# Two-layer squared-ReLU kernel: column-tiled warm-up, natural weight group only in block 0, no loads on the GpSimd queue

## The chip, the cores and the metric

The kernel runs on one core of one Trainium2 chip. The metric is the device time in microseconds (us), lower is better. Most executions of a kernel agree within 0.3%, so a change of a few tenths of a microsecond in 291 is read from repeated runs and, above all, from the trace, where single instructions have start times. All runs quoted here are with a granted TensorE clock of 0.999 to 1.0 in the mean.

Names: PE is TensorE, PEld its weight loads (LDWEIGHTS), ACT is ScalarE, DVE is VectorE, POOL is GpSimd, SP is SyncE. A name with a q at the end is that engine's sequencer, which issues DMAs. A *slot* is the time from the start of one 512-column matmul to the start of the next; w1n is the natural group's weight tile, loaded in slices of the contraction rows (four of 128 and a short one of 64, in two halves), w_h and w_x in the views are the row-pair weights `w1_h` and `w1_x`.

## The reference

```python
B, S, D, F = 1, 2048, 576, 4608          # all bf16
h = einsum("bsd,df->bsf", x, w1) + b1    # (2048, 4608)
h = relu(h) ** 2
out = einsum("bsf,fd->bsd", h, w2) + b2  # (2048, 576)
```

## The kernel before

The 2048 rows are cut into 4 blocks of 512. For each block, the first layer makes 36 tiles of 128 hidden features ("phase A"); for two blocks at a time the second layer follows. D is 576 = 9 x 64, so a tile needs 4.5 passes of 128 contraction rows. The kernel avoids the half-empty pass in two ways:

- 32 of the 36 tiles are made in *row pairs*: one tile in array rows 0 to 63 and another in rows 64 to 127, nine 64-row matmuls each, running side by side. A pair takes 9 slots. Its two weight halves come as two loads, "lower" and "upper".
- the other 4 tiles, the *natural group*, use 4 full 128-row passes each plus one 64-row pass shared by two: 16 + 2 = 18 slots for four tiles, as many as two row pairs.

```python
WARM = [512] * 6 + [128]
for i, n in enumerate(WARM):                      # keeps PE busy until x lands
    matmul(wps[:, 0:n], lhsT=ones[:, 0:P], rhs=ones[:, 0:n], start=True, stop=True)
# loads: x tiles 0, 3 and w1n slices 0..3 on SyncE, x tiles 1, 2 on ScalarE
...
nc.gpsimd.dma_start(out=b1_rows[0:NFT, :], in_=b1...)          # b1
for h in range(2):
    nc.gpsimd.dma_start(out=b2_col[h*DT:(h+1)*DT, :], in_=b2...)  # b2, twice 64 x 2 B
...
def a_rows(sb, ...):                              # row pairs j = 0..15
    for j in range(NJ):
        bx, by = psum(), psum()
        for i in range(NC):                       # 9 slots, two matmuls side by side
            matmul(bx, lhsT=w1_h[0:H, LO_C[i], jc], rhs=xT[0:H, LO_W[i], :])
            matmul(by, lhsT=w1_h[H:P, UP_C[i], jc], rhs=xT[H:P, UP_W[i], :])
        evac_h(sb, bx, G + j); evac_h(sb, by, G + NJ + j)   # ACT relu+b1, DVE square
# row weights, on SyncE, one lower and one upper load for each range of pairs:
# (0,1) w1n rest (1,2) (2,4) (4,6) (6,8) (8,10) (10,12) x block 1 (12,14) (14,16)
...
a_full(0, "k_outer"); a_rows(0, 12, 1)            # block 0: natural group first
a_rows(1); a_full(1, "rows_first")                # block 1: natural group last
phase_t(0)                                        # last 64 output columns, transposed
phase_b(0, ...); phase_b(1, ...)                  # the other 512 output columns
a_full(2, "g_outer"); a_rows(2)                   # block 2: natural group first
a_rows(3); a_full(3, "rows_first")                # block 3: natural group last
phase_t(2); phase_b(2, ...); phase_b(3, ...)
```

## Time and profile before

| | before |
|---|---|
| time, median of 3 runs | 291.73 us (291.54 to 291.87) |
| span of the profiled run | 289.8 us |
| PE busy | 285.1 us, 98% |
| one 512-column slot, start to start | 0.2157 us |

The page of the kernel before: the head, PE's busy time, and the chain that ended last by engine.

```profile
span 289.8 us, 4679 instructions
...
PE 285.1 (98%) x2017; PEld 133.7 (46%) x2032; DVE 79.5 (27%) x176; ACT 95.2 (33%) x152; POOL 2.8 (1%) x11
...
q0 software_dynamic: 96, 0.01, 0.0%
...
PE 98%; issue 0%; DVE 0%
```

The chain is PE from end to end: whatever is to be gained must be taken from PE's own sequence. The q0 line is the GpSimd queue with the three small loads (96 packets).

The timeline of the kernel before, PE only (start, duration, engine, line, operation, names, shapes), at the end of phase A of block 1: row pairs, natural group, transposed output.

```profile
72.16 0.38 PE L191 MATMUL ph<-xTw,w_h 64*128 64x512 bf16 x1
72.38 0.38 PE L204 MATMUL pn<-xTw,w1n 64*128 64x512 bf16 x1
72.38 0.38 PE L206 MATMUL pn<-xTw,w1n 64*128 64x512 bf16 x1
72.59 0.38 PE L204 MATMUL pn<-xTw,w1n 64*128 64x512 bf16 x1
72.59 0.38 PE L206 MATMUL pn<-xTw,w1n 64*128 64x512 bf16 x1
73.13 3.40 PE L210 MATMUL pn<-xTw,w1n 128*128 128x512 bf16 x15 [0.16 <-issue]
76.46 0.84 PE L272 MATMUL pt<-hT,w_sb 128*64 128x512 bf16 x6
```

From 72.38 to 76.46 are 4.08 us for 18 slots of 0.2157 us (3.88 us). The 0.20 us over are two changes of tile shape: 64-row tiles to the full array, and the full array to 64-column tiles. (The group shows 15 of 16 matmuls: the record of one beside such a change is missing.)

The start of the kernel before in PE's timeline: warm-up, transposes of x, first matmuls.

```profile
0.77 2.83 PE L63 MATMUL wps<-const-bfloat16-1.0 128*128 128x512 bf16 x7 [0.77 <-PEq L346]
3.49 1.25 PE L150 MATMUL tb<-ident,x_sb 128*128 128x128 bf16 x10
4.59 1.01 PE L228 MATMUL pn<-xTw,w1n 128*128 128x256 bf16 x4
```

Ten 128-column transposes from 3.49 to 4.59 are 0.11 us each; after 6.65 us the spacing in the trace is 0.056 us. PE works at half speed up to there. Below, this step from half to full speed is called the opening of the clock gate.

### The profile page before, as it was taken

To read this page: it belongs to the slowest core of one execution; us is meant where nothing else is said; L and a number is where in the kernel's file an instruction comes from. 1 tells how busy PE (TensorE), PEld (TensorE's weight loads), DVE (VectorE), ACT (ScalarE), POOL (GpSimd) and SP (SyncE) were. 2 spreads that over 40 slices of the span, in tenths; PEclk is the share of its full clock that TensorE was granted. 3 is DMA by queue.
4 is the path that set the end of the run, shared out by engine and by line. 5 is a ranking of instruction groups with operands and counts; after the bars stand their busy time and mean duration, and the time that the engine had idled before them with its cause. 6 is when DMAs were issued, how large, how long until landed. Compare 5 with 4: busy or idle time off the path is not lost.

```text
span 289.8 us, 4679 instructions
## 1 busy us (share of the span) xinstructions
PE 285.1 (98%) x2017; PEld 133.7 (46%) x2032; DVE 79.5 (27%) x176; ACT 95.2 (33%) x152; POOL 2.8 (1%) x11
## 2 busy tenths in 40 slices
PE   8999999999999999999999999999999999999996
PEld 5544444444444444444444444444445444444454
DVE  1644554444502100000025444444440000000001
ACT  2666666666500000000027666666670000000000
POOL 3000000000000000000000000000000000000000
PEclk9999999999999999999999999999999999999999
DMA  7999999400001000000000000000000200000000
GB/s 198 213 235 185 315 388 234 83 0 2 0 19 33 5 20 18 18 18 20 18 18 2 1 2 0 2 0 2 0 2 0 38 18 18 18 20 18 20 18 20
DMA packets 30581, 16.26 MB, mean 56 GB/s; under 512 B 14676, under 2 KB 30560, under 8 KB 30560
## 3 DMA queue, kind: packets, MB, share of 16 engines
q1 hardware_dynamic: 30176, 15.65, 21.7%
q8 instruction: 16, 0.26, 0.4%
q10 hardware_dynamic: 288, 0.30, 0.4%
q14 instruction: 5, 0.04, 0.0%
q0 software_dynamic: 96, 0.01, 0.0%
HBM read 11.36 MB, written 2.36 MB: 47 GB/s over the span
## 4 chain that ended last, share of the span: by engine, by line
PE 98%; issue 0%; DVE 0%
PE po L293 43%; PE ph L189 42%; PE pt L272 5%; PE pn L210 4%; PE pn L228 1%; PE wps L63 1%; PE tb L150 1%; PE ph L191 1%; PE pn L204 1%; DVE o_sb L295 0%; PE b1T_ps L167 0%; PE pn L206 0%
## 5 line engine op out<-in xcount | busy, mean ns | idle before, releaser
L191 PE MATMUL ph<-xTw,w_h 64*128 64x512 bf16 x576 | 124.6, 376 | 0.0
L189 PE MATMUL ph<-xTw,w_h 64*128 64x512 bf16 x576 | 124.6, 376 | 0.0
L293 PE MATMUL po<-w_sb,hT 128*128 128x512 bf16 (+2 forms) x600 | 123.8, 366 | 0.8 <-issue 0.3
L177 ACT ACTIVATE r<-ph,b1T 128x512 bf16<-128x512 f32 x128 | 81.0, 684 | 41.7 <-PE ph L191 41.7
L293 PEld LDWEIGHTS <-hT 128*128 128x128 bf16 x612 | 58.3, 98 | 66.7 <-issue 0.8
L189 PEld LDWEIGHTS <-w_h 64*128 64x128 bf16 x576 | 54.1, 94 | 68.3
L178 DVE TENSOR_TENSOR hT<-r 128x512 bf16<-128x512 bf16 x144 | 61.1, 425 | 75.9 <-ACT r L177 75.4
L191 PEld LDWEIGHTS <-w_h 64*128 64x128 bf16 x576 | 54.1, 94 | 0.0
L295 DVE TENSOR_TENSOR o_sb<-po,b_bc 128x512 bf16<-128x512 f32 (+2 forms) x17 | 11.2, 660 | 125.0 <-PE po L293 125.0
L177 ACT ACTIVATE r<-pn,b1T 128x512 bf16<-128x512 f32 x16 | 10.3, 687 | 68.7 <-PE pn L206 67.4
L272 PE MATMUL pt<-hT,w_sb 128*64 128x512 bf16 x144 | 15.9, 380 | 0.0
L272 PEld LDWEIGHTS <-w_sb 128*64 128x64 bf16 x144 | 8.0, 110 | 7.8 <-issue 0.8
L210 PE MATMUL pn<-xTw,w1n 128*128 128x512 bf16 x45 | 10.4, 379 | 0.4 <-issue 0.3
L210 PEld LDWEIGHTS <-w1n 128*128 128x128 bf16 x48 | 4.5, 98 | 6.0 <-issue 0.8
L275 ACT ACTIVATE oT<-pt,b2T 128x512 bf16<-128x512 f32 x2 | 1.4, 687 | 14.5 <-PE pt L272 14.5
L228 PE MATMUL pn<-xTw,w1n 128*128 128x256 bf16 x32 | 4.8, 304 | 0.0
L228 PEld LDWEIGHTS <-w1n 128*128 128x128 bf16 x32 | 3.4, 110 | 0.6
L63 PE MATMUL wps<-const-bfloat16-1.0 128*128 128x512 bf16 (+1 forms) x7 | 2.8, 581 | 0.8 <-PEq L346 0.8
L157 DVE COPY xTw<-tb 128x256 bf16<-128x256 bf16 x4 | 1.1, 292 | 6.6 <-PE tb L150 6.6
L120 DVE COPY xTw<-xTw 64x2048 bf16<-64x2048 bf16 x4 | 2.8, 690 | 0.2
L121 DVE COPY xTw<-xTw 64x2048 bf16<-64x2048 bf16 x4 | 2.7, 687 | 0.1
L159 ACT COPY xTw<-tb 128x256 bf16<-128x256 bf16 x4 | 1.3, 375 | 3.7 <-PE tb L150 3.7
(23 smaller groups left out, 16.9 us busy)
## 6 DMA issues: line engine op xcount, KB each, us to landing
w_sb<-in_w_dram SPq DMA_DIRECT2D x6, 864.0 KB, 9.6
w_h<-in_w_dram SPq DMA_DIRECT2D x14, 288.0 KB, 6.8
out_dram<-o_sb SPq DMA_DIRECT2D x15, 128.0 KB, 1.7
w_h<-in_w_dram SPq DMA_DIRECT2D x4, 144.0 KB, 3.6
w1n<-in_w_dram SPq DMA_DIRECT2D x4, 128.0 KB, 3.7
x_sb<-in_x_dram ACTq DMA_DIRECT2D x2, 144.0 KB, 2.8
x_sb<-in_x_dram SPq DMA_DIRECT2D x2, 144.0 KB, 3.3
out_dram<-ot SPq DMA_DIRECT2D x4, 64.0 KB, 1.8
```

The lines of the kernel that those rows point to most:

```text
L63: keep(nc.tensor.matmul(wps[:, 0:n], lhsT=ones[:, 0:P], rhs=ones[:, 0:n], start=True, stop=True))
L150: keep(nc.tensor.transpose(bank[:, slot, qc], xs[:, j, c0:c0 + P], ident[:]))
L177: keep(nc.scalar.activation(out=r[:], in_=bank[:], func=ACT.Relu, bias=b1T[:, ft:ft + 1], scale=1.0))
L178: keep(nc.vector.tensor_tensor(out=hTs[sb][:, ft, :], in0=r[:], in1=r[:], op=ALU.mult))
L189: keep(nc.tensor.matmul(bx[:], lhsT=w1_h[0:H, LO_C[i], jc], rhs=xT[0:H, LO_W[i], :], start=(i == 0), stop=(i == NC - 1)))
L191: keep(nc.tensor.matmul(by[:], lhsT=w1_h[H:P, UP_C[i], jc], rhs=xT[H:P, UP_W[i], :], start=(i == 0), stop=(i == NC - 1)))
L204: keep(nc.tensor.matmul(banks[2 * i][:], lhsT=w1n8[0:H, i, :], rhs=xT[0:H, SPC, :], start=start, stop=stop, skip_group_check=order == "k_o ...
L210: keep(nc.tensor.matmul(banks[g][:], lhsT=w1n[:, k, g * P:(g + 1) * P], rhs=xT[:, O + k, :], start=start, stop=stop))
L228: keep(nc.tensor.matmul(banks[g][:, hc], lhsT=w1n[:, k, g * P:(g + 1) * P], rhs=xT[:, O + k, hc], start=(h == 0 and k == 0), stop=False, s ...
L272: keep(nc.tensor.matmul(pt[h * DT:(h + 1) * DT, :], lhsT=w2_sb[:, ft, DM:D], rhs=hTs[sb + h][:, ft, :], start=(i == 0), stop=(i == NFT - 1)))
L293: keep(nc.tensor.matmul(po[:, 0:d1 - d0], lhsT=hT[:, ft, jj * P:(jj + 1) * P], rhs=w2_sb[:, ft, d0:d1], start=(i == 0), stop=(i == NFT - 1)))
L295: keep(nc.vector.tensor_tensor(out=o_sb[:, d0:d1], in0=po[:, 0:d1 - d0], in1=b2_bc[:, d0:d1], op=ALU.add))
```

## The change

The intent, as the diff shows it: the same array work with fewer changes of shape (the natural group stays in block 0 alone; in blocks 1 to 3 its four tiles become two more row pairs with their own weight tile `w1_x`), a warm-up in four 32-column tiles, and no load on the GpSimd queue. w2 comes in 9 chunks in place of 6. Cut to its core:

```diff
-    WARM = [512] * 6 + [128]
-    for i, n in enumerate(WARM):
-        keep(nc.tensor.matmul(wps[:, 0:n], lhsT=ones[:, 0:P], rhs=ones[:, 0:n], start=True, stop=True))
+    WARM = [512] * 6 + [64]
+    for n in WARM:
+        for c in range(0, P, 32):
+            keep(nc.tensor.matmul(wps[c:c + 32, 0:n], lhsT=ones[:, 0:32], rhs=ones[:, 0:n], start=True, stop=True))
...
-    nc.gpsimd.dma_start(out=b1_rows[0:NFT, :], in_=b1.rearrange("(ft p) -> ft p", p=P))
-    b2_col = ...; for h in range(2): nc.gpsimd.dma_start(out=b2_col[...], in_=b2[...])
+    nc.scalar.dma_start(out=b1_rows[0:NFT, :], in_=b1.rearrange("(ft p) -> ft p", p=P))
...
-    W2CH = 6
+    W2CH = 4
...
-        for j in range(NJ):
+        pairs = [] if sb == 0 else [(w1_x, j, j, G // 2 + j) for j in range(G // 2)]
+        pairs += [(w1_h, j, G + j, G + NJ + j) for j in range(NJ)]
+        for n, (w, j, fa, fb) in enumerate(pairs):
...                                             # a_full becomes a_first, block 0 only
+    for h in range(2):
+        load_w1x(nc.sync, h)                    # after the last row weights
+    for h in range(2):
+        keep(nc.sync.dma_start(out=b2_col[...], in_=b2[...]))
...
     a_rows(1)
-    a_full(1, "rows_first")
     phase_t(0)
...
-    a_full(2, "g_outer")
     a_rows(2)
...
     a_rows(3)
-    a_full(3, "rows_first")
```

More of the change, by code (lines that the diff above doesn't have):

```diff
@@ L68 @@
     w1_h = wpool.tile([P, NC, FH], BF16, name="w1_h")
+    w1_x = wpool.tile([P, NC, GW // 2], BF16, name="w1_x")
     w1_v = w1.rearrange("(c p) f -> p c f", p=H)
@@ L83, in load_w1, with load_w1x @@
                       in_=w1_v[:, :, GW + h * FH + j0 * P:GW + h * FH + j1 * P]))
+    def load_w1x(eng, h):
+        keep(eng.dma_start(out=w1_x[h * H:(h + 1) * H, :, :], in_=w1_v[:, :, h * GW // 2:(h + 1) * GW // 2]))
     load_x(nc.sync, 0)
@@ L97 @@
     nc.gpsimd.memset(b1_rows[:], 0.0)
-    nc.gpsimd.dma_start(out=b1_rows[0:NFT, :], in_=b1.rearrange("(ft p) -> ft p", p=P))
-    b2_col = const.tile([P, 1], BF16, name="b2_col")
-    for h in range(2):
-        nc.gpsimd.dma_start(out=b2_col[h * DT:(h + 1) * DT, :], in_=b2[DM:D].rearrange("(d o) -> d o", o=1))
-    b2T = const.tile([P, 1], FP32, name="b2T")
-    nc.gpsimd.tensor_copy(out=b2T[:], in_=b2_col[:])
+    nc.scalar.dma_start(out=b1_rows[0:NFT, :], in_=b1.rearrange("(ft p) -> ft p", p=P))
     warm = const.tile([P, 1], FP32, name="warm")
@@ L181, in a_rows @@
         xT = xT_blk[sb]
-        for j in range(NJ):
-            if j == dup_at:
+        pairs = [] if sb == 0 else [(w1_x, j, j, G // 2 + j) for j in range(G // 2)]
+        pairs += [(w1_h, j, G + j, G + NJ + j) for j in range(NJ)]
+        for n, (w, j, fa, fb) in enumerate(pairs):
+            if n == dup_at:
                 dup_windows(dup_sb)
@@ L188, in a_rows @@
             for i in range(NC):
-                keep(nc.tensor.matmul(bx[:], lhsT=w1_h[0:H, LO_C[i], jc], rhs=xT[0:H, LO_W[i], :],
+                keep(nc.tensor.matmul(bx[:], lhsT=w[0:H, LO_C[i], jc], rhs=xT[0:H, LO_W[i], :],
                                  start=(i == 0), stop=(i == NC - 1)))
-                keep(nc.tensor.matmul(by[:], lhsT=w1_h[H:P, UP_C[i], jc], rhs=xT[H:P, UP_W[i], :],
+                keep(nc.tensor.matmul(by[:], lhsT=w[H:P, UP_C[i], jc], rhs=xT[H:P, UP_W[i], :],
                                  start=(i == 0), stop=(i == NC - 1)))
-            evac_h(sb, bx, G + j)
@@ L194, in a_rows, with a_first, part @@
-            evac_h(sb, by, G + NJ + j)
-    def a_full(sb, order):
-        xT = xT_blk[sb]
-        banks = []
-        for g in range(G):
-            pool, tag = (ps_o, "po") if g < 2 else (ps_h, "ph")
-            banks.append(pool.tile([P, SB], FP32, name="pn", tag=tag))
-        def pair(i, start, stop):
+            evac_h(sb, bx, fa)
+            evac_h(sb, by, fb)
+    def a_first():
+        xT = xT_blk[0]
+        banks = [ps_o.tile([P, SB], FP32, name="pn", tag="po") for _ in range(2)]
+        banks += [ps_h.tile([P, SB], FP32, name="pn", tag="ph") for _ in range(2)]
+        tb_new = [ps_h.tile([P, 2, HS], BF16, name="tb", tag="ph") for _ in range(2)]
+        half_banks[1] = tb_new + tb_po
+        def part(h, k):
+            hc = slice(h * HS, (h + 1) * HS)
+            for g in range(G):
+                keep(nc.tensor.matmul(banks[g][:, hc], lhsT=w1n[:, k, g * P:(g + 1) * P], rhs=xT[:, O + k, hc],
+                                      start=(h == 0 and k == 0), stop=False, skip_group_check=True))
+        for j in range(2):
+            for k in range(NK):
+                x_transpose(j, k)
+        for j in range(2):
+            x_transpose(j, NK)
+        x_copies(0)
+        part(0, 0)
+        for k in range(NK + 1):
+            x_transpose(2, k)
+        part(0, 1)
+        part(0, 2)
+        for k in range(NK + 1):
+            x_transpose(3, k)
+        x_copies(1)
+        dup_windows(0)
+        part(0, 3)
+        part(1, 0)
+        make_b1T()
+        for k in range(1, NK):
+            part(1, k)
+        for i in (1, 0):
@@ L204, in pair @@
             keep(nc.tensor.matmul(banks[2 * i][:], lhsT=w1n8[0:H, i, :], rhs=xT[0:H, SPC, :],
-                             start=start, stop=stop, skip_group_check=order == "k_outer"))
+                                  start=False, stop=True, skip_group_check=True))
             keep(nc.tensor.matmul(banks[2 * i + 1][:], lhsT=w1n8[H:P, i, :], rhs=xT[H:P, E3, :],
-                             start=start, stop=stop, skip_group_check=order == "k_outer"))
-        def full(g, k, start, stop):
-            keep(nc.tensor.matmul(banks[g][:], lhsT=w1n[:, k, g * P:(g + 1) * P], rhs=xT[:, O + k, :],
-                             start=start, stop=stop))
@@ L213, in a_full @@
-        if order == "rows_first":
-            for i in (1, 0):
-                pair(i, True, False)
-            for g in (2, 3, 0, 1):
-                for k in range(NK):
-                    full(g, k, False, k == NK - 1)
-                evac_h(sb, banks[g], g)
-        else:
-            if order == "k_outer":
-                tb_new = [ps_h.tile([P, 2, HS], BF16, name="tb", tag="ph") for _ in range(2)]
-                half_banks[1] = tb_new + tb_po
-                def part(h, k):
-                    hc = slice(h * HS, (h + 1) * HS)
-                    for g in range(G):
-                        keep(nc.tensor.matmul(banks[g][:, hc], lhsT=w1n[:, k, g * P:(g + 1) * P],
-                                              rhs=xT[:, O + k, hc], start=(h == 0 and k == 0), stop=False,
-                                              skip_group_check=True))
-                for j in range(2):
-                    for k in range(NK):
-                        x_transpose(j, k)
-                for j in range(2):
-                    x_transpose(j, NK)
-                x_copies(0)
-                part(0, 0)
-                for k in range(NK + 1):
-                    x_transpose(2, k)
-                part(0, 1)
-                part(0, 2)
-                for k in range(NK + 1):
-                    x_transpose(3, k)
-                x_copies(1)
-                dup_windows(0)
-                part(0, 3)
-                part(1, 0)
-                make_b1T()
-                for k in range(1, NK):
-                    part(1, k)
-            else:
-                for g in (2, 3, 0, 1):
-                    for k in range(NK):
-                        full(g, k, k == 0, False)
-            for i in (1, 0):
-                pair(i, False, True)
-                evac_h(sb, banks[2 * i], 2 * i)
-                evac_h(sb, banks[2 * i + 1], 2 * i + 1)
@@ L261 @@
+                                  start=False, stop=True, skip_group_check=True))
+            evac_h(0, banks[2 * i], 2 * i)
+            evac_h(0, banks[2 * i + 1], 2 * i + 1)
     ft_order = list(range(G))
@@ L263 @@
         ft_order += [G + j, G + NJ + j]
-    t_order = ft_order[G:] + ft_order[:G]
     EDGES = [0, 384, 512]
@@ L269, in phase_t @@
         pt = ps_o.tile([P, SB], FP32, name="pt", tag="po")
-        for i, ft in enumerate(t_order):
+        for i, ft in enumerate(ft_order):
             for h in range(2):
@@ L307 @@
         load_w1(nc.sync, 1, j0, j1)
+    for h in range(2):
+        load_w1x(nc.sync, h)
+    b2_col = const.tile([P, 1], BF16, name="b2_col")
+    for h in range(2):
+        keep(nc.sync.dma_start(out=b2_col[h * DT:(h + 1) * DT, :], in_=b2[DM:D].rearrange("(d o) -> d o", o=1)))
+    b2T = const.tile([P, 1], FP32, name="b2T")
+    nc.gpsimd.tensor_copy(out=b2T[:], in_=b2_col[:])
     keep(nc.sync.dma_start(out=b2_bc[:], in_=b2.partition_broadcast(P)))
-    for c in (0, 3, 1, 4, 2, 5):
+    for c in (0, 1, 5, 2, 6, 3, 7, 4, 8):
         load_w2(c)
@@ L313 @@
     alloc_hT(0)
-    a_full(0, "k_outer")
+    a_first()
     a_rows(0, 12, 1)
```

## The prediction

> **What bounds the kernel now.** TensorE. The page has PE busy 98% of 289.8 us at a granted clock of 1.0; the chain of waits is 98% PE. In the timeline every 512-column slot starts 0.2157 us after the one before, whether it is one 128x128 matmul or two 64-row ones side by side.
>
> **What moves without changing the sum.** The natural group is 16 full and 2 paired slots: 18 slots, 3.88 us. In blocks 1 to 3 it becomes two row pairs, 2 x 9 = 18 slots. The extra LDWEIGHTS are hidden (0.09 us inside a slot).
>
> **What is removed.** Switches of tile shape. The Trainium skill, "TensorEngine Tiling (Array Packing)", "Key Properties", says a change of mode drains the engine; the trace agrees and gives the price. From the first natural pair of block 1 (72.38) to the first matmul of the transposed output (76.46) is 4.08 us against 3.88 for 18 slots: two switches, 0.10 us each. In block 2 the one switch back costs 0.105 us (146.52 to 150.51, 18 slots). Blocks 1 and 3 lose one switch each; block 2 only moves it. Gain: 0.2 us, all on the chain.
>
> **Start.** Warm-up runs from 0.77; six matmuls 0.427 us apart and a short one end as x tile 0 lands (3.45); transposes start at 3.49. Four 32-column tiles should run side by side, as the two 64-column tiles do in the transposed output (72 matmuls in 7.87 us), so six groups still take about 2.6 us, and a shorter last group plus one switch equals the old last matmul. No gain. Matmul spacing halves only at 6.65: until then the array is at half speed. The skill, "TensorE: Matmul & The Clock Gate", Part 1, describes such a gate. Column tiles might open it earlier, but loads cap that: w1n slice 2, used from 6.72, landed at 6.42, and x tile 3 at 6.04. An early gate brings the rest forward by about 0.2 us, no more. I give that one chance in four.
>
> **Loads.** b1, issued from ScalarE at about 1.6, delays its table load (1.63 to 2.91) by 0.4 us; its first copy is at 4.35, so nothing waits. The GpSimd queue's 96 packets took 1.2 us of engine time in total, under 0.1 us on each of 16 engines; taking them out may bring w1n forward by up to 0.1 us. The extra w1 load (0.59 MB) follows the last row weights (33.6) and lands well before block 1 (about 45). w2 ends before 57 and is first used at 76.
>
> **Sum.** -0.2 (switches), -0.1 (start, mean of the above): 291.4 us. Range 290.8 to 291.9. Faster by over 2%: 0.01; within 2%: 0.98; slower: 0.01.
>
> **What the profile would show.** The natural group's line in block 0 alone; five switches after block 0 in place of seven; block 1, first row matmul to transposed output, shorter by 0.1 us; row slots still 0.2157 us; warm-up in groups of four starting within some 10 ns, groups 0.427 us apart; first transpose at 3.4 to 3.6; queue 0 empty.
>
> **What would make it wrong.** Column tiles that run one after another at the low clock: +7 us. Warm-up that the gate doesn't count, so that full speed comes one window (3.4 us by the skill) later: up to +1.7 us. A gate that opens much earlier together with earlier loads: up to -1 us. Row weights late in block 1, seen as a PE wait on w1_x.

## The result, and the profile after

| | before | after |
|---|---|---|
| median of the fast runs | 291.35 us (291.08 to 291.87, 6 runs) | 292.25 us (291.62 to 292.33, 6 runs) |
| ratio | | 1.0024, 95% interval 1.0010 to 1.0038 |
| span of the profiled run | 289.8 us | 290.4 us |

A ratio is the mean time of one kernel's fast runs over that of the other's of the same rounds, so it is not quite the ratio of the medians quoted. The kernel is slower by a quarter of a percent: within 2%, but 0.9 us above the old median where 0.3 us less had been forecast, and outside the range (290.8 to 291.9).

Three stretches of each kernel, cut where the row pairs of block 0 begin and where the transposed output of block 1 begins (stretch, its length, then busy time of PE and the others, clock, DMA share, GB/s). The kernel before:

```profile
0.00:10.20 10.20, 9.43 (x64) 6.45 (x66) 3.07 (x9) 2.78 (x7) 2.76 (x11) 1.00 0.70 189
10.20:76.45 66.25, 66.09 (x597) 29.61 (x594) 31.06 (x73) 44.84 (x71) 0.00 (x0) 1.00 0.73 174
76.45:289.80 213.35, 209.57 (x1359) 97.64 (x1372) 45.39 (x95) 47.59 (x75) 0.00 (x0) 1.00 0.05 13
```

The kernel after:

```profile
0.00:9.50 9.50, 8.34 (x85) 5.45 (x87) 3.05 (x9) 2.78 (x7) 0.84 (x7) 1.00 0.68 182
9.50:77.20 67.70, 66.66 (x614) 29.62 (x610) 31.05 (x72) 44.08 (x71) 0.39 (x1) 1.00 0.79 182
77.20:290.40 213.20, 209.71 (x1393) 97.71 (x1404) 45.43 (x95) 48.11 (x76) 0.00 (x0) 1.00 0.05 13
```

(The clock column says 1.00 for the slow start too: the clock records begin only where full speed begins, at 6.65 us before and at 3.66 us after.) The start is 0.7 us shorter, the end 0.15 us shorter, and the middle, which should have been 0.1 us shorter, is 1.45 us longer. The page of the kernel after shows that the chain has left PE for the first time:

```profile
span 290.4 us, 4825 instructions
...
PE 94%; DMA 3%; SPq 2%; issue 0%; DVE 0%
PE po L270 43%; PE ph L191 24%; PE ph L193 22%; PE pt L249 5%; DMA w_h<-in_w_dram 2%; SPq L84 1%; DMA x_sb<-in_x_dram 1%; SPq L81 0%; SPq L77 0%; DVE o_sb L272 0%
```

The waits of PE's weight loads in the kernel after (who waits for what: us in total, times, longest):

```profile
PEld L193 <- DMA w_h<-in_w_dram: 2.0, 2, 1.2
...
PEld L150 <- DMA x_sb<-in_x_dram: 0.7, 1, 0.7
PEld L208 <- DMA w1n<-in_w_dram: 0.4, 1, 0.4
```

The same view of the kernel before has one wait for a DMA:

```profile
PEld L150 <- DMA x_sb<-in_x_dram: 0.5, 1, 0.5
```

The first of the two long waits, in PE's timeline of the kernel after; L191 is the lower half of a pair, L193 the upper half:

```profile
11.24 0.38 PE L191 MATMUL ph<-xTw,w_h 64*128 64x512 bf16 x1
11.24 0.38 PE L193 MATMUL ph<-xTw,w_h 64*128 64x512 bf16 x1
11.46 0.38 PE L191 MATMUL ph<-xTw,w_h 64*128 64x512 bf16 x1
12.54 0.39 PE L193 MATMUL ph<-xTw,w_h 64*128 64x512 bf16 x1 [0.71 <-ACT r L177]
12.54 0.39 PE L191 MATMUL ph<-xTw,w_h 64*128 64x512 bf16 x1
...
14.28 0.38 PE L193 MATMUL ph<-xTw,w_h 64*128 64x512 bf16 x1
14.28 0.38 PE L191 MATMUL ph<-xTw,w_h 64*128 64x512 bf16 x1
14.99 0.39 PE L193 MATMUL ph<-xTw,w_h 64*128 64x512 bf16 x1 [0.33 <-DMA w_h<-in_w_dram]
```

The second pair begins at 11.46; its upper half should start beside it and starts 1.08 us later. The bracket names ACT, which is the other thing that this matmul waits for; the weight-load view above gives the DMA, and the load landed at 12.49. From then on the halves run one slot apart. The third pair's upper half stalls again, up to 14.99. In the kernel before the second pair's halves start side by side, at 12.16 (here L189 is the lower half, L191 the upper):

```profile
12.16 0.38 PE L189 MATMUL ph<-xTw,w_h 64*128 64x512 bf16 x1
12.16 0.38 PE L191 MATMUL ph<-xTw,w_h 64*128 64x512 bf16 x1
```

Why does a weight load come late? The trace records when each of the 16 parts of a load raises the load's semaphore. (The Trainium skill, "DMA: Bandwidth & Descriptors", section "Why a DMA increments its semaphore by 16 and not by 1", says that the engines that share a DMA finish independently and that only the full 16 means that all data landed; the trace agrees, with 16 increments for each of these loads.) Worked out from those records, with the time at which PE would need the load if it had not stalled before (start of the rows plus 1.94 us for each pair):

```
load                        issued   15 of 16 landed   all landed   needed
before  pair 1, upper         7.00        10.24            10.54      12.16
        pairs 2-3, lower      7.68        11.88            11.90      14.10
        pairs 2-3, upper      8.36        13.54            13.61      14.10
after   pair 1, upper         7.28        10.57            12.49      11.46
        pairs 2-3, lower      7.96        12.44            13.73      13.40
        pairs 2-3, upper      8.64        13.64            14.94      13.40
```

(Pairs are counted from 0, so "pair 1" is the second.) In the kernel after fifteen parts of the load arrive as before and the sixteenth comes 1.9 us later; on the following loads the last part stays 1.3 us behind the others. It looks as if one DMA engine is behind (an inference, since the records don't name engines). The DMA records show what else was moved at that moment: one packet of 16 KB on queue 8, of the kind "instruction", started at 10.40 and took 0.92 us. In the kernel before the first such packet started at 15.90.

In both pages that queue has 16 packets, 0.26 MB in all. From the page of the kernel after:

```profile
PE 284.7 (98%) x2089; PEld 132.8 (46%) x2101; DVE 79.5 (27%) x176; ACT 95.0 (33%) x152; POOL 1.2 (0%) x8
...
q8 instruction: 16, 0.26, 0.3%
```

The Trainium skill, "Runtime: NRT & Kernel Launch", section "Instruction fetch mechanics", says that an engine's instructions are fetched in blocks of 16 KiB, 256 instructions. Sixteen such blocks are 4096 instructions, and only PE has so many (its two rows in the page after: 2089 and 2101). So these are PE's instructions. The traces agree: whatever the kernel, the sixth, seventh and eighth blocks start when 1435 to 1445, 1686 to 1691 and 1939 to 1947 PE instructions (matmuls and weight loads) have started, in all fourteen profiles. The new warm-up has 28 matmuls and 28 weight loads in place of 7 and 7: 42 PE instructions more at the very front.

### The profile page after: what moved, and what is told of

Same layout as the page of the kernel before. It is cut to its first block, busy times and chain, and to the rows that moved or that the text cites. A ratio compares the mean times of both kernels' runs of the same rounds, so it can differ in the third digit from the quotient of the medians.

```text
span 290.4 us, 4825 instructions
## 1 busy us (share of the span) xinstructions
PE 284.7 (98%) x2089; PEld 132.8 (46%) x2101; DVE 79.5 (27%) x176; ACT 95.0 (33%) x152; POOL 1.2 (0%) x8
## 4 chain that ended last, share of the span: by engine, by line
PE 94%; DMA 3%; SPq 2%; issue 0%; DVE 0%
PE po L270 43%; PE ph L191 24%; PE ph L193 22%; PE pt L249 5%; DMA w_h<-in_w_dram 2%; SPq L84 1%; DMA x_sb<-in_x_dram 1%; SPq L81 0%; SPq L77 0%; DVE o_sb L272 0%
## 5 line engine op out<-in xcount | busy, mean ns | idle before, releaser
L193 PE MATMUL ph<-xTw,w_h 64*128 64x512 bf16 x576 | 125.3, 376 | 1.0 <-ACT r L177 0.7
L191 PE MATMUL ph<-xTw,w_h 64*128 64x512 bf16 x576 | 125.3, 376 | 0.0
L177 ACT ACTIVATE r<-ph,b1T 128x512 bf16<-128x512 f32 x140 | 88.5, 684 | 110.9 <-PE ph L193 87.3
L191 PEld LDWEIGHTS <-w_h 64*128 64x128 bf16 x576 | 54.0, 94 | 35.3
L193 PEld LDWEIGHTS <-w_h 64*128 64x128 bf16 x576 | 54.0, 94 | 34.6 <-DMA w_h<-in_w_dram 2.0
L191 PE MATMUL ph<-xTw,w_x 64*128 64x512 bf16 x54 | 12.1, 376 | 0.0
L193 PE MATMUL ph<-xTw,w_x 64*128 64x512 bf16 x54 | 12.1, 376 | 0.0
L191 PEld LDWEIGHTS <-w_x 64*128 64x128 bf16 x54 | 5.0, 94 | 4.5 <-issue 0.4
L193 PEld LDWEIGHTS <-w_x 64*128 64x128 bf16 x54 | 5.0, 94 | 2.1
L208 PE MATMUL pn<-xTw,w1n 128*128 128x256 bf16 x32 | 4.2, 273 | 0.3 <-DMA w1n<-in_w_dram 0.2
L64 PE MATMUL wps<-const-bfloat16-1.0 128*32 128x512 bf16 (+1 forms) x28 | 2.8, 575 | 0.8 <-PEq L327 0.8
L208 PEld LDWEIGHTS <-w1n 128*128 128x128 bf16 x32 | 2.9, 98 | 0.9 <-DMA w1n<-in_w_dram 0.4
L177 ACT ACTIVATE r<-pn,b1T 128x512 bf16<-128x512 f32 x4 | 2.4, 687 | 2.1 <-PE pn L234 2.1
```

What stands on the lines that cost most here:

```text
L64: keep(nc.tensor.matmul(wps[c:c + 32, 0:n], lhsT=ones[:, 0:32], rhs=ones[:, 0:n], start=True, stop=True))
L177: keep(nc.scalar.activation(out=r[:], in_=bank[:], func=ACT.Relu, bias=b1T[:, ft:ft + 1], scale=1.0))
L191: keep(nc.tensor.matmul(bx[:], lhsT=w[0:H, LO_C[i], jc], rhs=xT[0:H, LO_W[i], :], start=(i == 0), stop=(i == NC - 1)))
L193: keep(nc.tensor.matmul(by[:], lhsT=w[H:P, UP_C[i], jc], rhs=xT[H:P, UP_W[i], :], start=(i == 0), stop=(i == NC - 1)))
L208: keep(nc.tensor.matmul(banks[g][:, hc], lhsT=w1n[:, k, g * P:(g + 1) * P], rhs=xT[:, O + k, hc], start=(h == 0 and k == 0), stop=False, s ...
```

## The experiments

Theory A: the 42 extra instructions bring the first fetch of PE's instructions forward into the loads of the first row weights; it occupies one of the DMA engines that also carry a sixteenth of each weight load, and PE stalls. As first stated, it also held that the column tiles open PE's clock gate early, which removes 0.7 us of slack. Rival B: the gate opens by chance, not by the tile shape. Rival C: the stall comes from the moved loads, since SyncE's later issues came 0.28 us later in the kernel after.

The table collects what the profiles show; times in us. "Full speed" is where the trace's clock record begins, or in brackets, where the records lack it, where matmul spacing halves. "Rows to output" runs from the first row matmul of block 0 to the first transposed-output matmul of block 1: 66.25 where block 1 still has the natural group and 66.14 where it hasn't, if nothing stalls. "Lost" is what is over that.

| profile | warm-up instructions | first fetch | full speed | rows start | rows to output | lost |
|---|---|---|---|---|---|---|
| before | 14 | 15.90 | 6.65 | 10.22 | 66.25 | 0 |
| before_again | 14 | 15.55 | 4.25 | 9.90 | 66.24 | 0 |
| e6_before_loads | 14 | 14.45 | 5.83 | 9.85 | 66.25 | 0 |
| e5_before_rows | 14 | 15.23 | 5.48 | 9.70 | 66.14 | 0 |
| e2_after_fullwarm | 14 | 13.33 | 5.56 | 9.75 | 66.14 | 0 |
| e2_again | 14 | 15.99 | 6.71 | 10.44 | 66.14 | 0 |
| e8_fullwarm_split | 14 | 13.14 | (5.1) | 9.50 | 66.46 | 0.3 |
| e4_after_onecol | 14 | 14.48 | 4.07 | 9.29 | 66.70 | 0.6 |
| e9_after_col28 | 28 | 11.47 | 3.48 | 9.24 | 68.39 | 2.3 |
| e1_before_colwarm | 56 | 12.02 | 6.52 | 10.24 | 66.25 | 0 |
| after | 56 | 10.40 | 3.66 | 9.51 | 67.73 | 1.6 |
| after_again | 56 | 10.54 | (5.8) | 9.98 | 67.24 | 1.1 |
| e3_after_fullwarm28 | 56 | 10.16 | 3.40 | 9.56 | 67.18 | 1.0 |
| e7_after_col112 | 112 | 7.96 | 4.17 | 10.49 | 66.33 | 0.2, and 1.2 before the rows |

The landing records of all fourteen profiles, read in the same way, tie the late part to the fetch. Before the first fetch starts, no load of w1n or of row weights up to 24 us has its last part more than 0.45 us behind the fifteenth; from one of the first three loads that land after that start, the last part is 0.7 to 1.9 us behind, and it stays more than 0.5 us behind for one to nine loads. So it is in the kernel before as well (0.7 us, on loads that land from 19.45), where these loads have slack. An estimate from the traces fits the size: a load of 288 KB is 18 KB for each of 16 parts, and such loads land about 1.2 us apart, so 16 KB more on one engine is about 1.1 us.

### e1: only the column-tiled warm-up, in the kernel before

```diff
-    WARM = [512] * 6 + [128]            # full array, 7 matmuls
+    WARM = [512] * 6 + [64]             # four 32-column tiles, 28 matmuls
```

> The kernel before with the column-tiled warm-up alone (56 warm-up instructions on TensorE in place of 14; loads, natural groups as before). Theory A: the column tiles make TensorE reach full speed by about 3.7 us in place of 6.65; the 42 extra instructions bring the first 16 KB instruction fetch on queue 8 forward from 15.9 to about 10 to 11 us; it holds up one of the 16 DMA engines, so the row-weight load for the upper half of the second pair lands about 2 us after its other 15 parts, and PE stalls 1 to 1.6 us near 12.5 us. Span 0.5 to 1.2 us longer than before. Rival B (the clock gate follows a free-running window, not the tile shape): full speed comes anywhere from 3.2 to 6.7 us. Rival C (the stall comes from moving b1 to ScalarE's queue, which pushed SyncE's later issues back by 0.28 us): no stall here, span not longer than before.

Measured: 292.30 us (4 runs, 291.58 to 292.54) against 291.50; ratio 1.0025, interval 1.0008 to 1.0043. The warm-up alone makes the kernel slower by as much as the whole change does, and so rival C is not needed. But the profile fell on the fastest of the four runs (291.58 us, span 289.8; the others had 290.3 to 290.8). In it the gate opened at 6.52, not at 3.7, the fetch came at 12.02, and nothing stalled: the last parts were 1.1 us behind from pairs 4 and 5 on (landed at 15.54, needed at about 18.0), not on the second pair. The half of theory A on the gate failed at once: these column tiles did not bring full speed early. That the three slower runs stalled was not seen, since they have no trace.

### e2 and e2_again: the kernel after with the old warm-up

```diff
-    WARM = [512] * 6 + [64]             # 28 matmuls of 32 columns
+    WARM = [512] * 6 + [128]            # 7 matmuls of 128 columns
```

> The kernel after with the old full-array warm-up (7 matmuls). Theory A: full speed near 6.65 us, first instruction fetch back at about 15 to 16 us, no PE stall in block 0; 0.2 us faster than before from the two tile switches saved. Rival B: full speed may come at 3.2 to 3.7 us in this kernel too, then 0.7 to 0.9 us faster than before. Rival C: the stall near 12.5 us stays.

Measured: 290.91 us (290.84 to 291.05) against 291.50; ratio 0.9982, interval 0.9967 to 0.9997.

> The kernel after with the old 14-instruction warm-up, again, on the same chip as the kernel after: 0.3 to 0.6 us faster than before, 0.8 to 1.3 us faster than after; first fetch at 13 to 16 us.

Measured on another chip: 291.24 us (290.71 to 291.51) against 291.53; ratio 0.9986, interval 0.9974 to 0.9998. The profile has the first fetch at 15.99 and no wait for row weights. Its PE weight-load waits, whole but for "issue":

```profile
...
PEld L149 <- DMA x_sb<-in_x_dram: 0.9, 1, 0.9
...
```

Everything in the change except the warm-up is worth about 0.15%, and the warm-up turns that into a loss of about 0.2%. e2 beats the kernel before in both trials, and the kernel after in the second, the only one in which both ran (292.16).

### e3: the old tile shape with as many instructions as the new one

```diff
-    WARM = [512] * 6 + [64]             # 28 matmuls of 32 columns, four side by side
+    WARM = [112] * 28                   # 28 matmuls of the full array, same total columns
```

> The kernel after with a full-array warm-up of the same total columns cut into 28 matmuls of 112 columns: 56 instructions without column tiles. Theory A: full speed near 6.65 us as in before; the instruction fetch comes at 10 to 12 us; PE starts the rows at 10.2 and stalls by 0.3 to 1 us near 12.5 us: slower than e2 by that. If the fetch has nothing to do with the stall: as fast as e2. Rival B: the time of full speed is independent of the tile shape and the number of instructions.

Measured: 291.84 us (291.68 to 292.50) against 291.50 for before and 290.91 for e2, all on one chip; ratio 1.0021 to before, interval 1.0004 to 1.0039. e3 and e2 differ in nothing but the cut of the warm-up into instructions (and its total, 3136 columns in place of 3200, about 0.05 us at the slow clock). The fetch came at 10.16 and PE stalled at the third pair (timeline, PE):

```profile
13.44 0.38 PE L190 MATMUL ph<-xTw,w_h 64*128 64x512 bf16 x1
14.47 0.39 PE L192 MATMUL ph<-xTw,w_h 64*128 64x512 bf16 x1 [0.66 <-DMA w_h<-in_w_dram]
```

The load it waited for (pairs 2-3, upper) had 15 parts by 13.43 and the last at 14.43. So it is the number of instructions, not the column tiles. The gate opened at 3.40 here, with the old tile shape: the expectation of 6.65 failed, so an early opening doesn't need column tiles.

### e4: one 32-column tile alone, 14 instructions

```diff
-        for c in range(0, P, 32):
-            keep(nc.tensor.matmul(wps[c:c + 32, 0:n], lhsT=ones[:, 0:32], rhs=ones[:, 0:n], ...))
+        keep(nc.tensor.matmul(wps[0:32, 0:n], lhsT=ones[:, 0:32], rhs=ones[:, 0:n], ...))
```

> The kernel after with one 32-column tile alone in the warm-up, 14 instructions. Theory A for the fetch: it comes at 15 to 16 us and PE does not stall by over 0.3 us in block 0. If the column shape by itself opens the gate: full speed near 3.7 us and about 0.8 us faster than before, the best of the four. If the gate counts how much of the array is active (a quarter here): full speed at 6.65 us or later, like e2 or up to 1.7 us slower. Rival B: no difference from e2 beyond chance.

Measured: 291.00 us (290.66 to 291.24); ratio 0.9984, interval 0.9969 to 0.9999: as fast as e2. With the fetch at 14.48 there is no 1 us stall, but 0.6 us are lost to the third pair all the same (more than the 0.3 us allowed for): its upper load landed at 13.68, with 15 parts at 13.65, and was needed at 13.17. The sixteenth part was 0.03 us behind the fifteenth, so no single part was held up: this isn't the fetch. Rows that start at 9.29 outrun the loads, so an early gate gives back most of what it wins.

### e5 and e6: the row pairs alone, the loads alone

```diff
 e5 = before + natural group in block 0 only, w1_x, W2CH = 4   (old warm-up, old b1/b2 loads)
 e6 = before + b1 on ScalarE, b2 late on SyncE                  (all else old)
```

> The kernel before with the natural group limited to block 0 alone (with its extra weight load, chunk size and order of the transposed output); old warm-up, b1 and b2 still on GpSimd's queue. If the gain is the two saved tile switches: faster than before by 0.2 us (0.1 in block 1, 0.1 in block 3), seven switches after block 0 become five, start unchanged. If e2's gain of 0.5 us came from the rows too, it is faster by 0.4 us or more.

> The kernel before with only the b1 and b2 loads moved off GpSimd's queue. If the loads are worth nothing: the same as before within 0.1 us. If the rest of e2's gain (0.3 us beyond the switches) is theirs: faster by about 0.3 us, seen as w1n slice 2 and x tile 3 landing earlier (before: 6.42 and 6.04). Rival C for the stall: a PE stall near 12.5 us appears; by the fetch theory none appears, since the warm-up has 14 instructions.

Measured, with 5 rounds: e5 291.12 us against 291.28, ratio 0.9998, interval 0.9985 to 1.0010; e6 291.40 us, ratio 1.0008, interval 0.9996 to 1.0021. Neither is separated from before by its time. e5's trace shows the saved change of shape. At the end of block 1 (timeline, PE) the row pairs lead straight into the transposed output:

```profile
75.53 0.38 PE L195 MATMUL ph<-xTw,w_h 64*128 64x512 bf16 x1
75.53 0.38 PE L197 MATMUL ph<-xTw,w_h 64*128 64x512 bf16 x1
75.84 0.62 PE L253 MATMUL pt<-hT,w_sb 128*64 128x512 bf16 x4
```

75.53 to 75.84 is a slot plus 0.09 us, one change in place of two, and rows to output is 66.14 against 66.25: 0.11 us, as predicted.

e6 disposes of rival C: SyncE's fourth w1n load was issued at 3.71 in place of 3.09, later than in the kernel after, and PE didn't stall. (The cause of that delay is in the trace: the fourth w1n load now uses the semaphore that x tile 1 used, and waits for it to land; b1 has taken one of the eight that the loads of SyncE and ScalarE go round.) What the moved loads do bring is w1n slice 2 earlier: it landed at 5.95 to 6.47 in the four profiles with loads on GpSimd's queue and at 5.69 to 6.09 in the ten without. That helps only where the gate opens early. The two parts' ratios do not add up to e2's 0.9982 and 0.9986; with intervals of 0.0012 either way this stays open.

### e7 and e9: more and fewer instructions in the same warm-up time

```diff
 e7:  WARM = [224] * 14, four 32-column tiles each        # 112 instructions
 e9:  WARM = [512] * 6 + [64], two 64-column tiles each   #  28 instructions
```

> The kernel after with the column-tiled warm-up cut finer: 14 groups of 224 columns, 112 instructions in the same time. By the fetch theory the first 16 KB fetch moves further forward with the 56 extra instructions, from about 10 us to 6 to 8 us, and holds up loads of that time (w1n slices or the first row weights), so PE stalls earlier and in another place, with little or no stall at 12.5 us. If the stall in after has another cause: it stays near 12.5 us. The clock gate opens at 3.4 to 6.7 us whatever the instruction count.

> The kernel after with two 64-column tiles in the warm-up, 28 instructions, between e2's 14 and after's 56. By the fetch theory the first fetch comes between theirs, at 11 to 14 us, later than the load for the second pair and with less harm: stalls of 0 to 0.7 us; time between e2 and after. If column tiles as such cost the time: as slow as after.

e7 measured 291.64 us against 291.28; ratio 1.0012, interval 0.9997 to 1.0028, so its time is not clearly different. Its trace is the clearest for the theory: the fetch moved to 7.96, and the load it held up was another one, the lower half of the short w1n slice (15 parts at 8.34, the last at 10.00), for which PE stalls before the rows. From its weight-load waits:

```profile
PEld L232 <- DMA w1n<-in_w_dram: 1.3, 1, 1.3
```

The row weights then found PE late, and nothing was lost at 12.5.

e9 measured 291.84 us with a scatter of its own, 291.00 to 292.83 (6 runs), against 291.53; ratio 1.0010, interval 0.9992 to 1.0029. "Between e2 and after" holds for the median, but not for its profile, which is the worst of all (2.3 us lost; the waits for row weights are the first two lines below). The fetch came at 11.47, into the loads for pairs 2 and 3, whose last parts landed 1.5 and 1.7 us after the fifteenth, while the rows had started early, at 9.24.

```profile
PEld L193 <- DMA w_h<-in_w_dram: 1.5, 2, 1.3
PEld L191 <- DMA w_h<-in_w_dram: 1.1, 1, 1.1
...
PEld L208 <- DMA w1n<-in_w_dram: 0.3, 1, 0.3
```

So half the instructions are not half the harm, and the fetch does not follow their number alone: it came earlier here than in e1's profile (12.02), which has twice as many but a late gate. What counts is which load the fetch hits and how soon that load is needed.

### e8: the third chunk split

```diff
-    for (j0, j1) in [(0, 1), (1, 2), (2, 4), (4, 6), ...
+    for (j0, j1) in [(0, 1), (1, 2), (2, 3), (3, 4), (4, 6), ...     # with e2's warm-up
```

> A version meant to beat both: after with the old 14-instruction warm-up and the third row-weight chunk split in two, so that the weights of the third pair land earlier (e4 stalled 0.34 us on them at 13.73 when the gate opened early). Expected: first fetch at 13 to 16 us, no PE stall in block 0 at any gate time, 0.5 to 0.9 us faster than before; up to 0.3 us faster than e2 where the gate opens early, the same where it opens late.

Measured: 291.07 us (290.76 to 291.25) against 291.28; ratio 0.9994, interval 0.9982 to 1.0007. The aim failed. The third pair's weights did land earlier (12.13, in e2 13.55), but the fetch, at 13.14, now hit the loads of pairs 4 and 5 and PE stalled at 17.59. The stall moved by two pairs. Nothing shows e8 to be better than e2: its interval overlaps both of e2's, which are from other chips.

### before_again and after_again: the same kernels once more

> The kernel before, unchanged, against itself: shows the noise (ratio 1.000 within 0.0013) and another profile with its own gate time. If the gate follows a free-running window, full speed comes anywhere from 3.2 to 6.7 us; where it comes before 5 us the rows start near 9.3 to 9.6 in place of 10.2 and the span is 289.2 to 289.4 in place of 289.8, with no PE stall above 0.4 us in block 0, since the first fetch stays at 13 to 16 us. If the tile shape set the gate: 6.5 us again.

> The kernel after, unchanged. Slower than before by 0.5 to 0.9 us in the median. In its profile: with an early gate a fetch near 10 us and PE stalls of 1 to 1.6 us in all, span 290.1 to 290.8; with a late gate (after 5.5 us) a fetch at 11 to 12 us, no stall and a span of about 289.6, as in e1's profile. If the gate is set by the column tiles: 3.7 us again.

before_again: 291.48 us against 291.53, ratio 0.9994, interval 0.9982 to 1.0006, which is the noise of such a comparison. Its gate opened at 4.25 with the old warm-up; the rows started at 9.90, later than the 9.3 to 9.6 expected, because w1n slice 2 landed at 6.35. after_again: 292.16 us (291.74 to 292.57) against 291.53, ratio 1.0018, interval 1.0005 to 1.0030. The slowdown is confirmed in a second set of runs.

My expectation for a late gate failed in after_again. PE reached full speed at about 5.8, and the kernel still lost 1.1 us. The profiles of before_again and after_again make a clean pair as to slack, though the whole change lies between them: rows start at 9.90 and 9.98; the fetch starts at 15.55 and 10.54; lost are 0 and 1.1 us. An early gate is not needed for the stall.

## Why the prediction was wrong

- **"What is removed: Switches of tile shape ... Gain: 0.2 us"** was right in size: 0.11 us in block 1 (66.25 to 66.14). From the transposed output of block 1 to PE's last matmul, with block 3 in between, PE takes 210.40 us before and 210.29 us after, another 0.11 us.
- **"What moves without changing the sum"** was right: slots of 0.216 us, no wait for `w1_x` in block 1.
- **"Start ... No gain"** for the warm-up is the step that failed. Its array time was costed correctly: the four tiles run side by side, groups 0.427 us apart, as expected. What was left out is the other thing a matmul is, an instruction to be fetched. The 42 instructions brought the first fetch from 13.1 to 16.0 us (all profiles with 14) to 10.2 to 12.0 us (all with 56), and PE lost 1.0 to 1.6 us in the three such profiles whose fetch came before 10.6. In the profile of the kernel after these 1.6 us outweighed what was won: 0.7 us at the start and 0.2 us in changes of shape. The page on the runtime cited above had the pieces, and adds that the fetch goes over a DMA queue while the engine executes. It calls the cost of a block boundary "mostly hidden". The block size agrees with the traces (packets of 16,384 bytes). Here the cost stayed hidden where the loads had slack (before: none of it lost) and not where they had none (after: 1.6 us).
- **"What would make it wrong"** named late row weights, but in block 1 and for `w1_x`. The row weights of block 0 were never compared with the time at which they are needed. The profile before had the numbers: pair 1 had 1.6 us to spare, and pairs 2-3 only 0.5 us (13.61 against 14.10), while the sixteenth part's delay in the kernel after was 1.3 to 1.9 us.
- **"An early gate brings the rest forward by about 0.2 us, no more"** was too small: rows started at 9.24 to 9.56 in five profiles (after, e3, e4, e8, e9; full speed at 3.4 to 5.1), 0.7 to 1.0 us before the 10.22 of the profile before. The cap was taken from landings of one profile (w1n slice 2 at 6.42), which was among the slowest of the fourteen. How much of this gain is luck stays open. The tile shape doesn't fix the time: full speed came at 3.40 to 6.71 us with full-array warm-ups and at 3.48 to 6.52 with column tiles, and the same kernel had 6.65 and 4.25 (before) or 3.66 and about 5.8 (after). But it came before 4.2 us in five of the seven profiles with a changed warm-up and in none of the seven with the old one, so that the new one shifts the odds is not excluded. The skill, "TensorE: Matmul & The Clock Gate", Part 1, says that the gate looks at a free-running window of 3413 ns. The traces agree: where the record of full speed is there, it lasts either 283.31 or 286.72 us, and these differ by 3.41 us.

What is shown: the number of warm-up instructions alone, with the same tile shape, makes e2 into e3, 0.9 us slower in the medians; the fetch moves with it; the loads around the fetch have fifteen parts on time and one late; PE waits for that load. What is inferred: that the fetch and the late part share one DMA engine, since the records at hand don't name engines. What stays open: which of the untraced slow runs of e1 and e9 stalled where; how e2's gain splits between rows and loads; why the first fetch scatters by 2.9 us (13.1 to 16.0) among kernels with the same 14 warm-up instructions; and why a part can be 1.9 us late beside a packet of 0.92 us.

## What to carry to other kernels

Instructions are data too: cutting the same array time into four times as many instructions at the front of a kernel moved the first instruction fetch forward here by 1 to 6 us, and a fetch among loads with little slack went with a late sixteenth of each of them, which delays the whole load. Before changing the start of a kernel that is fed just in time, list for each early load when it landed and when its first user needs it; what the start gains beyond the smallest slack is lost again in the wait for that load. When an optimisation of the warm-up is judged by one profile, take several: here full speed came anywhere in a range of 3.3 us, and 2.4 us apart in two profiles of the same kernel.

## What the Trainium skill lacked or had wrong

- "Runtime: NRT & Kernel Launch", "Instruction fetch mechanics", calls the cost of a 16 KiB boundary "mostly hidden". Here each block's packet took 0.88 to 1.32 us in the first two of every profile read, the last part of the first weight load that the first block met came 0.7 to 1.9 us after the other fifteen, and PE lost up to 1.6 us in the kernel after (2.3 us in e9). The page doesn't say that a fetch competes with the kernel's own loads.
- "CRC Debugging", "Comparing the Two Runs", puts the sequencers' instruction refills on queue 14. In these traces PE's sixteen 16 KB blocks were all on queue 8; queue 14 carried packets of the kind "instruction" too, of 8 KB, five in every span.
- "TensorE: Matmul & The Clock Gate", Part 1, holds as far as these runs go: full speed began 2.6 to 5.9 us after the first warm-up matmul (0.77), at 3.40 to 6.71 us. Whether the tile shape or the number of instructions shifts the odds within that range is not settled here.
- "TensorEngine Tiling (Array Packing)", "Key Properties", says that a change of tiling mode drains the engine but gives no price. Here a change cost 0.09 to 0.10 us beyond the normal slot (0.306 to 0.312 us from start to start, where no record is missing).
